# GpSimd refines the reciprocal root of 28 head pairs, and the low half of the first relu stands ahead of a weight join

## The chip, the cores and the metric

The kernel runs on one core of a Trainium2 chip. Its engines are TensorE (PE: matrix multiplications; PEld: loading their weights), VectorE (DVE), ScalarE (ACT), GpSimd (POOL) and SyncE (SP, which here only issues DMAs). Each engine works through its own queue in order; they wait for one another by semaphores. The metric is the device time of one execution in microseconds. Before the change it was 823.23 us, the median of three runs (823.1 to 826.74).

## The reference

Linear attention without softmax, RMS normalisation, then token mixing of rank 32 and a feed-forward network with residuals:

```
kv  = einsum('bhsd,bhse->bhde', k, v)          # 8 batches, 8 heads, 576 rows, 64
out = einsum('bhsd,bhde->bhse', q, kv)
rms = sqrt(mean(out * out, axis=-1) + 1e-06)
x   = out / rms * g_norm                       # heads side by side: 8 x 576 x 512
u   = x + (x^T @ U @ V)^T                      # mixes the 576 rows, rank 32
y   = u + relu(u @ w_ch1) @ w_ch2              # 512 -> 2048 -> 512
```

All in fp32.

## The kernel before, in words

**Products.** An fp32 operand is split into a high half and a low half that TensorE multiplies at its full rate; a product takes three multiplications (high·high, high·low, low·high), each 128x512. The weights of the feed-forward network are split on the way in: a chunk f of them goes through decode steps that the order table calls A, D0, D1, B, D2, H and L. D2 is the join on VectorE (L166, `dec<-raw,top`, 128x1024), H the high half on ScalarE (L260), L the low half on VectorE (L264). `m2D2` is the join of chunk 2.

**Attention.** A step deals with a batch b and a pair of heads p, 32 pairs in all. The four pairs of batch 0 have code of their own (`first_pair`, with its own refinement at L993 to L996, untouched). For the other 28, `stats_parts` (L359 to L373) makes the reciprocal root of the mean square, ten numbers in each of 128 partitions:

- `red` (VectorE): sums of squares; `ta`, `hf` (ScalarE): the root, and −1/2 of the mean square;
- `rc` (VectorE, L370): r0, the reciprocal of the root;
- `na`, `nb`, `nw` (VectorE, L371 to L373): one Newton step, half = (r0·half·r0 + 1.5)·r0.

`mul_step` (VectorE, L384, or L387 for the two heads apart) multiplies the attention output by `half`. From its result TensorE makes the product with U (`t_product`, L410 and L413), and `turn_step` transposes it (VectorE, L400) and sends it through DRAM (`xd`, SP's DMAs at L403 and L405) into the layout of the token mixing, which comes back as `ut` (TensorE L507, VectorE L510, then the split of the row into halves at L451 and L452).

**Feed-forward.** Rows are dealt with in blocks of 512 columns; for a block, chunk f of 16: `ffn1` (L530 to L532) fills a bank `h`, ScalarE makes the high half of its relu (L542, `hh`), VectorE the low half (L547, `hl = max(h, 0) − hh`), and `ffn2` (L554) accumulates. In the first chunks of block 0 there is one bank `h`: chunk f+1 can be begun when the low half of chunk f (`hl0` for chunk 0) has read it. From about 333 us to the end, after three blocks, the rest goes through a Strassen-like scheme (L717, L819, with VectorE's L839 and L841 finishing rows).

**What sets the order.** Up to the end of block 0 two tables (`ORDER0`, `ORDER1`) name every step of that stretch, and each engine's queue has its steps in the order of the table. After that TensorE's order is written out, and that of the other engines comes from a scheduler that simulates the program. The program names a step by letters and the chunk or pair: `f1a` is the first quarter of ffn1 of chunk 1, `hh0` and `hl0` are the relu halves of chunk 0; `na4` is the first refinement step of batch 1's pair 0.

**GpSimd before.** It zeroes buffers at the start, and from then on issues DMAs that store weights to DRAM for the later scheme: a copy `begun<-hh` of 128x1 waits for a chunk's `hh` (L1118 in block 0, L1292 in blocks 1 and 2), three issues of quarters follow (L643, `wd<-ws`), and issues of combinations of weights (L677, `wd<-sh` or `wd<-dec`), which VectorE and ScalarE make at L659, L668, L674 and L675.

Of the kernel before, what the change touches and what calls it, by code (L numbers as in the profile page):

```python
# [16 lines left out]
ALU = mybir.AluOpType  # L17
# [36 lines left out]
tx0 red1 w1B hf1 w1D2 kv3 ta1 t4c0 rc1 w1H t4s0 kv2 nw1 kvb3 w1L wd3 kvb2 mul1 out2 w2A w2D0 out3 lw3 lw2 lw1 sq2 w2D1  # L54
cA tx1 red2 sq3 cD0 ta2 tr1 hf2 red3 t4c1 w2B tr0 rc2 eA t4s1 mix0 nw2 mix1 ta3 cD1 uh0 rc3 mul2 hf3 uh1 nw3 cB tx2
eD0 m2A mul3 tr2 lw4 t4c2 ul1 r0 tx3 t4s2 te0 eD1 sh0 ul0 r1 t4c3 cD2 mix2 te1 tr3 t4s3 cH w2D2 uh2 mix3 m2D0 kv4 uh3
ul2 r3 eB ul3 kvb4 te3 w2H kvc4 f0d eD2 sh1 sh3 m2D1 f0b eH w2L f0c m2B cL f0a eL out4 hh0 m2D2 m3A r2 hl0 m2H m3D0
f1a sq4 f1b m2L te2 f1d lw0 sh2 m3D1 f1c m4A red4 y0 hh1 m4D0 m3B hl1 ta4 m4D1 hf4 f2a m3D2 f2c rc4 m3H sl0 f2d na4
sl1 nb4 sl3 nw4 sl2 f2b mul4 m4B y1 m3L hh2 hl2 m5A m4D2 f3b m5D0 m4H f3a f3d trn4 f3c m4L y2 hh3 m5D1 m6A hl3 m5B
m6D0 f4a m6D1 f4c m5D2 f4b f4d m5H y3 hh4 m5L m6B hl4 m7A m6D2 f5a m7D0 m6H  # L60
# [34 lines left out]
def build(ctx: ExitStack, tc: tile.TileContext, kv_in, kvt0_in, kvt_in, q_in, uv_in, g_in, w_in, out):  # L95
    nc = tc.nc
# [262 lines left out]
    def stats_parts(b, p):  # L359

        NS = 2 * NT
        sums, half, r0, ta = [sm.tile([P, NS], F32, name=n) for n in ("sums", "half", "r0", "ta")]
        xv = state[b, p]["x2"].rearrange("p i (h e) -> p i h e", e=D)
        state[b, p]["r"] = half.rearrange("p (i h) -> p i h", h=2)

        return dict(
            red=lambda: nc.vector.tensor_reduce(out=sums.rearrange("p (i h) -> p i h", h=2), in_=xv, axis=AX.X, op=ALU.add),
            ta=lambda: nc.scalar.activation(out=ta, in_=sums, func=AF.Sqrt, scale=1.0 / D, bias=eps[:, 0:1]),
            hf=lambda: nc.scalar.activation(out=half, in_=sums, func=AF.Identity, scale=-0.5 / D, bias=eps[:, 1:2]),
            rc=lambda: nc.vector.reciprocal(out=r0, in_=ta),  # L370
            na=lambda: nc.vector.tensor_tensor(out=ta, in0=r0, in1=half, op=ALU.mult),  # L371
            nb=lambda: nc.vector.tensor_tensor(out=ta, in0=ta, in1=r0, op=ALU.mult),
            nw=lambda: nc.vector.scalar_tensor_tensor(out=half, in0=ta, scalar=1.5, in1=r0, op0=ALU.add, op1=ALU.mult))  # L373

    def stats_step(b, p):
        for what in stats_parts(b, p).values():
            what()
# [570 lines left out]
    def spread_v(n, eng):  # L948
# [4 lines left out]
        out=uv, in_=uvraw.bitcast(U32).rearrange("p (n t) -> p n t", t=2)[:, :, 1].bitcast(F32), func=AF.Abs)  # L953
# [113 lines left out]
    def second_batch():  # L1067
        own = {}

        def kv():  # L1070
            own["kv"] = [bank()[:, 0:D] for r in range(2)]
            kv_product(1, 0, own["kv"])
            load_kv(1, 1)

        def o():
            out_product(1, 0, (bank(), bank()))
            load_q(1, 1)
            for n, what in stats_parts(1, 0).items():
                step[f"{n}4"] = what

        step.update(kv4=kv, kvb4=lambda: kv_move(1, 0, own["kv"]), kvc4=lambda: kv_add(1, 0, own["kv"]), out4=o, sq4=lambda: squares(1, 0),
                    mul4=lambda: mul_step(1, 0), trn4=lambda: turn_step(1, 0))
# [55 lines left out]
    def stretch(name, before, now, after):  # L1138
# [17 lines left out]
        def o():  # L1156
            out_product(*now, (place("one"), place("two")))
            behind_turn(load_q, *now)
            new_steps(squares_parts(*now))
            new_steps(stats_parts(*now))  # L1160
# [230 lines left out]
```

## Time and profile before

| | |
|---|---|
| median of three runs | 823.23 us (823.1 to 826.74) |
| span of the profiled execution | 820.8 us |
| TensorE busy | 812.3 us, 99% |
| VectorE busy | 590.0 us, 72% |
| ScalarE busy | 438.9 us, 53% |
| GpSimd busy | 83.0 us, 10% |

The page has no time of the profiled execution beside its span; the median of the runs is 2.4 us above the span. An engine's busy time counts the union of its instructions, DMA issues among them for GpSimd. A matmul's end is modelled, so that consecutive ones overlap in a timeline: a 128x512 one is shown with 0.39 us and the next begins 0.23 us after it.

### The profile page before, as it was taken

What the parts mean: (1) busy time and instruction counts of PE and PEld (TensorE: products, weight loads), DVE (VectorE), ACT (ScalarE), POOL (GpSimd) and SP (SyncE); (2) the same over time, 40 slices, a digit from 0 to 9 for tenths busy, and PEclk for the clock granted to TensorE, in tenths of its full rate; (3) what the DMA queues carried; (4) which work ended last, traced back from release to release, by engine and by line L of the source; (5) the groups of instructions that cost most, each with busy time, mean ns of one, the idle gap of its engine ahead of it and who ended that gap; (6) DMA issues with size and microseconds to landing.
All of it is one profiled execution on the core that took longest, in us unless ns stands there. A gap on an engine that the chain in (4) does not pass through costs nothing.

```text
span 820.8 us, 15247 instructions
## 1 busy us (share of the span) xinstructions
PE 812.3 (99%) x5940; PEld 669.8 (82%) x5940; DVE 590.0 (72%) x1044; ACT 438.9 (53%) x782; POOL 83.0 (10%) x159
## 2 busy tenths in 40 slices
PE   9899999999999999999999999999999999999998
PEld 8688888878888888888888888888888888888887
DVE  5999995887876788558867688678538933682376
ACT  6869773344433545456645664656246624543462
POOL 3002232345321221000000000000000000000000
PEclk9999999999999999999999999999999999999999
DMA  9985778788896777577778768675555675555554
GB/s 344 415 352 162 231 238 259 256 272 269 271 318 226 240 254 233 167 264 246 251 241 287 230 212 294 222 246 196 193 205 193 204 272 202 206 179 186 199 205 154
DMA packets 64824, 196.87 MB, mean 240 GB/s; under 512 B 8176, under 2 KB 25840, under 8 KB 54000
## 3 DMA queue, kind: packets, MB, share of 16 engines
q1 hardware_dynamic: 55648, 166.40, 59.7%
q0 software_dynamic: 8960, 29.37, 10.6%
q8 instruction: 47, 0.77, 0.4%
q14 instruction: 25, 0.20, 0.1%
q10 hardware_dynamic: 144, 0.13, 0.0%
HBM read 145.27 MB, written 50.59 MB: 239 GB/s over the span
## 4 chain that ended last, share of the span: by engine, by line
PE 93%; DVE 4%; DMA 1%; issue 1%; ACT 1%; POOL 0%; SPq 0%; DVEq 0%; ACTq 0%; POOLq 0%
PE yy L717 28%; PE yy L819 26%; PE y L554 15%; PE h L530 5%; PE h L531 5%; PE h L532 5%; PE ya L769 2%; PE pp L313 1%; PE pp L333 1%; PE h L859 1%; PE h L313 1%; DMA wd<-dec 1%; PE pp L410 1%; DMA q_sb<-q_in 1%; PE big L333 1%
## 5 line engine op out<-in xcount | busy, mean ns | idle before, releaser
L717 PE MATMUL yy<-uc,wt 128*128 128x512 f32 x1008 | 233.5, 391 | 0.0
L717 PEld LDWEIGHTS yy<-uc,wt 128*128 128x128 f32 x1008 | 188.2, 188 | 39.3
L819 PE MATMUL yy<-dec,wt 128*128 128x512 f32 x468 | 113.7, 391 | 0.0
L554 PE MATMUL y<-hh,ws 128*128 128x512 f32 x336 | 113.1, 394 | 0.0
L819 PE MATMUL yy<-hh,wt 128*128 128x512 f32 x312 | 103.4, 391 | 0.0
L819 PEld LDWEIGHTS yy<-dec,wt 128*128 128x128 f32 x468 | 87.4, 188 | 18.2
L708 DVE TENSOR_TENSOR hl<-hk,hh 128x512 fp32r<-128x512 f32 x72 | 48.1, 687 | 43.9 <-ACT hh L747 43.7
L708 DVE TENSOR_TENSOR dec<-hk,dec 128x512 fp32r<-128x512 f32 x72 | 49.0, 687 | 36.9 <-ACT dec L747 36.5
L554 PEld LDWEIGHTS y<-hh,ws 128*128 128x128 f32 x336 | 63.1, 188 | 13.6
L819 PEld LDWEIGHTS yy<-hh,wt 128*128 128x128 f32 x312 | 58.6, 188 | 12.2
L530 PE MATMUL h<-ut,ws 128*128 128x512 f32 x168 | 66.5, 396 | 0.0
L531 PE MATMUL h<-ut,ws 128*128 128x512 f32 x168 | 65.6, 390 | 0.0
L532 PE MATMUL h<-ut,ws 128*128 128x512 f32 x168 | 65.6, 390 | 0.0
L554 PE MATMUL y<-hl,ws 128*128 128x512 f32 x168 | 65.5, 390 | 0.0
L819 PE MATMUL yy<-hl,wt 128*128 128x512 f32 x156 | 60.8, 390 | 0.0
L747 ACT CAST dec<-hk 128x512 fp32r<-128x512 f32 x72 | 44.2, 620 | 30.5 <-PE yy L819 15.6
L747 ACT CAST hh<-hk 128x512 fp32r<-128x512 f32 x72 | 44.1, 622 | 27.5 <-PE yy L819 22.9
L705 ACT COPY sp<-yy 128x1024 f32<-128x1024 f32 x35 | 35.5, 1014 | 35.5 <-PE yy L717 27.5
L730 ACT ACTIVATE hk<-hk 128x1024 f32<-128x1024 f32 x24 | 25.5, 1061 | 37.7 <-DVE hk L729 37.6
L542 ACT ACTIVATE hh<-h 128x512 fp32r<-128x512 f32 x48 | 28.4, 591 | 30.7 <-PE h L532 30.6
L547 DVE SCALAR_TENSOR_TENSOR hl<-h,hh 128x512 fp32r<-128x512 f32 x48 | 32.8, 683 | 10.1 <-ACT hh L542 9.8
L532 PEld LDWEIGHTS h<-ut,ws 128*128 128x128 f32 x168 | 31.6, 188 | 6.8
(246 smaller groups left out, 1349.5 us busy)
## 6 DMA issues: line engine op xcount, KB each, us to landing
wt<-wd SPq DMA_DIRECT2D x84, 1024.0 KB, 4.9
kv_sb<-kv_in SPq DMA_DIRECT2D x29, 512.0 KB, 6.1
raw<-w_in SPq DMA_DIRECT2D x14, 1023.6 KB, 15.4
wd<-dec POOLq DMA_DIRECT2D x44, 256.0 KB, 5.0
wd<-ws POOLq DMA_DIRECT2D x42, 256.0 KB, 4.8
q_sb<-q_in SPq DMA_DIRECT2D x29, 288.0 KB, 5.9
ut<-xd SPq DMA_DIRECT2D x28, 288.0 KB, 4.5
out<-x SPq DMA_DIRECT2D x23, 256.0 KB, 4.5
```

The lines of the kernel that those rows point to most:

```text
L530: nc.tensor.matmul(h, lhsT=w1s[f][0][:, d, :], rhs=uh[d], start=(n == 0), stop=False)
L531: nc.tensor.matmul(h, lhsT=w1s[f][0][:, d, :], rhs=ul[d], start=False, stop=False)
L532: nc.tensor.matmul(h, lhsT=w1s[f][1][:, d, :], rhs=uh[d], start=False, stop=(n == ND - 1))
L542: last["relu"] = nc.scalar.activation(out=last["hh"], in_=h, func=AF.Relu)
L547: last["low"] = nc.vector.scalar_tensor_tensor(out=hl, in0=h, scalar=0.0, in1=last["hh"].bitcast(F32), op0=ALU.max, op1=ALU.subtract)
L554: nc.tensor.matmul(acc, lhsT=w2s[f][w][:, c, :], rhs=h[:, cols], start=(f == 0 and w == 0 and h is hh), stop=(f == NF - 1 and w == 1))
L705: last["unit"] = nc.scalar.copy(out=pair_bank("P6") if name == "P1" else spare(name), in_=acc)
L708: return nc.vector.tensor_tensor(out=out, in0=a, in1=b, op=ALU.subtract)
L717: nc.tensor.matmul(acc[:, i], lhsT=w[:, ws_, e * P:(e + 1) * P], rhs=u[:, e, us], start=name in ("P1", "P5") and e == 0 and k == 0, stop=e ...
L730: last["unit"] = nc.scalar.activation(out=to, in_=to if other else acc, func=AF.Relu)
L747: last["unit"] = nc.scalar.copy(out=hh, in_=src)
L819: nc.tensor.matmul(acc[:, c], lhsT=w[:, ws_, c * P:(c + 1) * P], rhs=h, start=name in ("P1", "P5") and kk == 0 and i == 0, stop=kk == KEEP ...
```

## The change

Two edits. In `ORDER0`, `hl0` moves from behind `m2D2 m3A r2` to directly behind `hh0`. In `stats_parts`, `na` and `nb` go from VectorE to GpSimd, and `nw`, one VectorE operation that adds 1.5 and multiplies by r0, becomes two GpSimd operations. The lines of the kernel behind L373 have a number higher by one after the change.

```diff
-ul2 r3 eB ul3 kvb4 te3 w2H kvc4 f0d eD2 sh1 sh3 m2D1 f0b eH w2L f0c m2B cL f0a eL out4 hh0 m2D2 m3A r2 hl0 m2H m3D0
+ul2 r3 eB ul3 kvb4 te3 w2H kvc4 f0d eD2 sh1 sh3 m2D1 f0b eH w2L f0c m2B cL f0a eL out4 hh0 hl0 m2D2 m3A r2 m2H m3D0
...
             rc=lambda: nc.vector.reciprocal(out=r0, in_=ta),
-            na=lambda: nc.vector.tensor_tensor(out=ta, in0=r0, in1=half, op=ALU.mult),
-            nb=lambda: nc.vector.tensor_tensor(out=ta, in0=ta, in1=r0, op=ALU.mult),
-            nw=lambda: nc.vector.scalar_tensor_tensor(out=half, in0=ta, scalar=1.5, in1=r0, op0=ALU.add, op1=ALU.mult))
+            na=lambda: nc.gpsimd.tensor_tensor(out=ta, in0=r0, in1=half, op=ALU.mult),
+            nb=lambda: nc.gpsimd.tensor_tensor(out=ta, in0=ta, in1=r0, op=ALU.mult),
+            nw=lambda: (nc.gpsimd.tensor_scalar(out=ta, in0=ta, scalar1=1.5, scalar2=None, op0=ALU.add),
+                        nc.gpsimd.tensor_tensor(out=half, in0=ta, in1=r0, op=ALU.mult)))
```

TensorE's order stays as it is. VectorE's queue at the first chunk, before (L921 is the end of the weights of chunk 0, L166 the join m2D2, L547 hl0, L264 the low half of chunk 2's weights):

```order
L921 TENSOR_TENSOR w2s_563<-dec,w2s_563 128x512
L166 SCALAR_TENSOR_TENSOR dec<-raw_206,top 128x1024
L547 SCALAR_TENSOR_TENSOR hl<-h,hh 128x512
L155 TENSOR_SCALAR dec<-dec 128x256
L156 TENSOR_SCALAR dec<-dec 128x1024
L264 TENSOR_TENSOR ws_613<-dec,ws_613 128x1024
```

and after the change:

```order
L922 TENSOR_TENSOR w2s_563<-dec,w2s_563 128x512
L548 SCALAR_TENSOR_TENSOR hl<-h,hh 128x512
L166 SCALAR_TENSOR_TENSOR dec<-raw_206,top 128x1024
L155 TENSOR_SCALAR dec<-dec 128x256
L156 TENSOR_SCALAR dec<-dec 128x1024
L264 TENSOR_TENSOR ws_613<-dec,ws_613 128x1024
```

The low half now stands ahead of the join, and nothing else moves there. GpSimd's queue in block 0 around the stores that follow the copy at 109 us, before:

```order
L1118 COPY begun<-hh 128x1
L643 DMA wd_117<-ws_722 128x2x256
L643 DMA wd_119<-ws_722 128x2x256
L643 DMA wd_120<-ws_780 128x2x256
L1118 COPY begun<-hh 128x1
```

and after, with the refinement of pair (1,3) (its r0 is r_1375):

```order
L1119 COPY begun<-hh 128x1
L644 DMA wd_117<-ws_723 128x2x256
L644 DMA wd_119<-ws_723 128x2x256
L644 DMA wd_120<-ws_781 128x2x256
L371 TENSOR_TENSOR ta<-r_1375,half 128x10
L372 TENSOR_TENSOR ta<-ta,r_1375 128x10
L373 TENSOR_SCALAR ta<-ta 128x10
L374 TENSOR_TENSOR half<-ta,r_1375 128x10
L1119 COPY begun<-hh 128x1
```

The four operations stand behind three DMA issues. In block 1, at pair (3,0) (r_2433), GpSimd's queue before:

```order
L1292 COPY begun<-hh 128x1
L643 DMA wd_135<-ws_1275 128x2x256
L643 DMA wd_138<-ws_1345 128x2x256
L643 DMA wd_141<-ws_1345 128x2x256
L677 DMA wd_125<-sh 128x512
L677 DMA wd_126<-sh 128x512
```

and after:

```order
L371 TENSOR_TENSOR ta<-r_2433,half 128x10
L1293 COPY begun<-hh 128x1
L644 DMA wd_135<-ws_1277 128x2x256
L644 DMA wd_138<-ws_1348 128x2x256
L644 DMA wd_141<-ws_1348 128x2x256
L372 TENSOR_TENSOR ta<-ta,r_2433 128x10
L678 DMA wd_125<-sh 128x512
L678 DMA wd_126<-sh 128x512
L373 TENSOR_SCALAR ta<-ta 128x10
L374 TENSOR_TENSOR half<-ta,r_2433 128x10
```

The copy and five issues now stand between the four operations of one pair. VectorE's queue at the same pair, after, from its reciprocal to its multiplication (L385):

```order
L370 RECIPROCAL r_2433<-ta 128x10
L548 SCALAR_TENSOR_TENSOR hl<-h,hh 128x512
L676 TENSOR_TENSOR sh<-st,sh 128x2x256
L548 SCALAR_TENSOR_TENSOR hl<-h,hh 128x512
L660 TENSOR_TENSOR st<-ws_813 128x512
L660 TENSOR_TENSOR st<-ws_893 128x512
L669 TENSOR_TENSOR st<-st 128x256
L385 TENSOR_TENSOR x_88<-x_88,half 128x640
```

Before, the multiplication and the transposition stood ahead of the second `hl` there; now that `hl`, both L660 and an L669 stand ahead of it.

## Rows read from the trace of the kernel before

**Rows 1.** The page: busy time, share and count of each engine; the chain's shares by engine.
```profile
PE 812.3 (99%) x5940; PEld 669.8 (82%) x5940; DVE 590.0 (72%) x1044; ACT 438.9 (53%) x782; POOL 83.0 (10%) x159
...
PE 93%; DVE 4%; DMA 1%; issue 1%; ACT 1%; POOL 0%; SPq 0%; DVEq 0%; ACTq 0%; POOLq 0%
```

**Rows 2.** Busy time in two stretches: start:end, length, then busy us of each engine.
```profile
0.00:36.70 36.70, 31.88 (x328) 27.59 (x328) 27.07 (x76) 26.31 (x65) 6.43 (x31) 1.00 0.97 375
36.70:820.80 784.10, 780.46 (x5612) 642.17 (x5612) 562.93 (x970) 412.55 (x718) 76.56 (x128) 1.00 0.70 234
```

**Rows 3.** The chain of waits from 30 to 62 us: start, us, what.
```profile
36.11 0.61 DVE hl L547
...
36.77 0.50 PE h L530
```

**Rows 4.** Timeline, ScalarE, VectorE, TensorE: start, us, engine, line, operation, shapes, [idle before].
```profile
34.70 0.60 ACT L542 ACTIVATE hh<-h 128x512 fp32r<-128x512 f32 x1
...
34.89 1.22 DVE L166 SCALAR_TENSOR_TENSOR dec<-raw,top 128x1024 uint32<-128x1024 uint32 x1
...
41.01 0.68 DVE L547 SCALAR_TENSOR_TENSOR hl<-h,hh 128x512 fp32r<-128x512 f32 x1
...
42.31 0.39 PE L530 MATMUL h<-ut,ws 128*128 128x512 f32 x1
```

**Rows 5.** Groups by line and form, VectorE, one of three alike.
```profile
L371 DVE TENSOR_TENSOR ta<-r,half 128x10 f32<-128x10 f32 x28 | 4.7, 168 | 1.4
```

**Rows 6.** Timeline, GpSimd's copy alone and beside a VectorE join.
```profile
77.08 0.18 POOL L1118 COPY begun<-hh 128x1 f32<-128x1 f32 x1 [4.03 <-ACT hh L542]
...
95.16 1.22 DVE L166 SCALAR_TENSOR_TENSOR dec<-raw,top 128x1024 uint32<-128x1024 uint32 x1
...
95.44 0.97 POOL L1118 COPY begun<-hh 128x1 f32<-128x1 f32 x1 [4.35 <-ACT hh L542]
```

**Rows 7.** Timeline around pair (1,0), VectorE and TensorE.
```profile
43.41 0.21 DVE L370 RECIPROCAL r<-ta 128x10 f32<-128x10 f32 x1
...
44.43 0.89 DVE L387 TENSOR_TENSOR x<-pp,half 128x320 f32<-128x320 f32 x2
...
46.37 0.69 DVE L547 SCALAR_TENSOR_TENSOR hl<-h,hh 128x512 fp32r<-128x512 f32 x1
...
47.75 0.39 PE L530 MATMUL h<-ut,ws 128*128 128x512 f32 x1
```

**Rows 8.** Timeline around pair (1,3), GpSimd, VectorE, TensorE.
```profile
109.93 2.17 POOL L643 DMA_DIRECT2D wd<-ws  x3
...
111.73 0.82 DVE L384 TENSOR_TENSOR x<-x,half 128x640 f32<-128x640 f32 x1
...
128.61 0.82 DVE L510 TENSOR_TENSOR ut<-pp,ut 128x288 f32<-128x288 f32 x2 [5.41 <-DMA ut<-xd]
...
130.94 0.47 PE L531 MATMUL h<-ut,w1s 128*128 128x512 f32 x1
```

**Rows 9.** Timeline around pair (3,0), GpSimd, VectorE, TensorE.
```profile
197.16 0.82 DVE L384 TENSOR_TENSOR x<-x,half 128x640 f32<-128x640 f32 x1
...
198.28 0.43 PE L410 MATMUL pp<-x,uf 128*32 128x128 f32 x8
...
199.35 1.27 DVE L659 TENSOR_TENSOR st<-ws 128x512 f32<-128x512 f32 x2
...
199.56 1.12 POOL L677 DMA_DIRECT2D wd<-sh  x2 [0.51 <-DVE hl L547]
...
200.66 1.56 DVE L668 TENSOR_TENSOR st<-st 128x256 f32<-128x256 f32 x4
```

**Rows 10.** Timeline at 421 us, VectorE and TensorE.
```profile
421.27 0.83 DVE L384 TENSOR_TENSOR x<-x,half 128x640 f32<-128x640 f32 x1
...
422.01 1.27 DVE L839 SCALAR_TENSOR_TENSOR x<-x,g_sb,yy 128x1024 f32<-128x1024 f32 x1
...
422.82 0.43 PE L410 MATMUL big<-x,uf 128*32 128x128 f32 x8
```

## The prediction

> **What bounds the kernel now.** I read the page's first part first, then its chain, then the busy time by stretch, then the timelines around each place that the change touches. The first row shows TensorE busy for 812.3 us of a span of 820.8 us, VectorE for 590.0 us, ScalarE for 438.9 us and GpSimd for 83.0 us; the chain of work that ended last is TensorE for 93% of the span and VectorE for 4% [rows 1]. The table of stretches says where the 4% lie: up to 36.70 us TensorE works 31.88 us, and in the 784.10 us behind that it works 780.46 us, at a granted clock of 1.00 [rows 2]. So from the second FFN chunk on all that can be won is 784.10 − 780.46 = 3.6 us, and every delay that reaches TensorE is paid in full, for there is no later idle time in which it is made good. VectorE's 72% is an average and is no bound anywhere after 36.70 us; what matters of it is when its queue, which runs in order, lets single results out.
>
> The last VectorE piece of the chain is the low half of the first relu, 36.11 to 36.72 us, and TensorE's second chunk starts at 36.77 us [rows 3]: the bank `h` is free for chunk 1 only when hl0 has read it.
>
> **Part 1, hl0 ahead of m2D2.** The high half hh0 runs on ScalarE from 34.70 for 0.60 us, so it ends at 35.30; the join m2D2 starts on VectorE at 34.89 for 1.22 us, and hl0 stands behind it [rows 4]. In the new order hl0 starts at hh0's end plus the 0.05 us that a hand-over takes in rows 3 (36.72 to 36.77), so near 35.35, and ends near 36.0 instead of 36.72: TensorE's chunk 1 starts some 0.7 us sooner. But VectorE, which is back to back here, now idles from 34.9 until 35.35 for hh0, some 0.45 us, and the join starts at 35.95 and not at 34.89. All that stands behind it on VectorE (one decode step, then the low half of chunk 2's weights after ScalarE's high half of them) is late by 0.3 to 0.7 us, down to hl1, which ran at 41.01 for 0.68 us. hl1 lets TensorE begin chunk 2 at 42.31, 0.62 us after hl1's end [rows 4]; with TensorE 0.7 us early and hl1 0.7 us late, hl1 would end at 42.4 and chunk 2 begin near 42.45: +0.14 us. The gain is spent one chunk later. Its bounds are −0.7 (hl1 doesn't slip) and +0.3 (it slips by a whole 0.9).
>
> **Part 2, what goes.** Three VectorE instructions for each of 28 pairs go, 84 in all; the first kind takes 168 ns (28 of them 4.7 us), the other two read alike [rows 5], so 84 × 0.168 = 14.1 us of VectorE's 590.0. VectorE isn't the bound after 36.70 us, so this is worth nothing in itself.
>
> **Part 2, what comes.** Four GpSimd operations of 128x10 for each pair, and two hand-overs between engines (the reciprocal to GpSimd, `half` back to VectorE's multiplication), where before there was none. The trace has no GpSimd arithmetic of this size. The nearest row is the copy of 128x1: 0.18 us when undisturbed, 0.97 us when it starts at 95.44 beside a VectorE join that runs from 95.16 for 1.22 us [rows 6]. The copy then ends at 96.41, 0.03 us after the join ends at 96.38: it seems to have been held until the join was over. So one operation costs 0.18 to 0.97 us. I take 0.25, near the undisturbed end, because at the places that count below VectorE itself stands waiting for the result, and there is nothing beside which to be held. A chain is then 4 × 0.25 + 3 × 0.05 between them + 2 × 0.05 hand-overs = 1.25 us, against 0.5 on VectorE, and the multiplication that waits for it holds all of VectorE's queue. In most pairs the reciprocal stands 0.7 us or more ahead of the multiplication, with other work between, and TensorE's consumer is microseconds later; those I cost at nothing. Four places are different.
>
> On the copy's two prices the Trainium skill bears: "GPSIMD Engine Reference", § 8 Key points, says that GpSimd shares its SBUF interfaces with VectorE and contends with VectorE instructions that have two SBUF inputs, and that elementwise work is structurally about twice as fast on VectorE. The 0.97 beside a join of two SBUF inputs agrees with the first. By the second an operation would be 2 × 0.168 = 0.34 us (an estimate from that page's factor), and a chain 1.6 us instead of 1.25.
>
> *Pair (1,0), 43 us.* The reciprocal runs from 43.41 for 0.21 us and the multiplications start at 44.43; hl2 stands behind them at 46.37 (0.69 us) and TensorE's chunk 3 follows at 47.75 [rows 7]. The chain ends at 43.62 + 1.25 = 44.87, so multiplication, weights and hl2 are 0.45 us later. In the new order these are already late by part 1. hl2's end has 0.69 us to TensorE; a slip of 0.45 on top of 0.7 uses it up and passes 0.45 on: **+0.45** (0 to +1).
>
> *Pair (1,3), 110 us.* On GpSimd the four operations stand behind a copy and three DMA issues of the weight stores; the issues run from 109.93 for 2.17 us, until 112.10. The chain ends near 113.3; the multiplication was at 111.73: +1.55 us. From it the result goes through the transposition, SP's DMAs to and from DRAM, and comes back for the token mixing, at 128.61, before which VectorE waited 5.41 us for the DMA; two operations later TensorE begins the row at 130.94, which is the second matmul group of block 1 and takes 0.47 us in place of its usual 0.39 because it already waits a little [rows 8]. So all of it arrives: **+1.5** (0.5 if VectorE's order makes some of it good, 2.5 if the operations cost 0.5).
>
> *Pair (3,0), 197 us.* Here GpSimd's order puts the copy, three store issues and two `sh` issues between the four operations. The two `sh` issues run from 199.56 for 1.12 us, until 200.68; the last two operations end near 201.25. The multiplication was at 197.16 and lasts 0.82, and TensorE uses its result at 198.28, 0.3 us after its end [rows 9]. That is 4.1 − 0.3 = +3.8 us. VectorE's new order sets a floor: the multiplication now stands behind two operations of L659 (1.27 us together) and one of L668 (1.56 for four) [rows 9], 1.66 us, so at least +1.4. The issues wait in the program on semaphores of earlier DMAs, which need not slip by the 2.1 us that TensorE is late by then; if they don't, 3.8 − 2.1 = 1.7. I take the middle of 1.7 and 3.8: **+2.8** (1.4 to 5.9, where GpSimd has a further 2 us of issues to wait for).
>
> *421 us.* VectorE's new order puts L839 (1.27 us, at 422.01) ahead of the multiplication at 421.27, whose result TensorE takes at 422.82 [rows 10]. If L839's input is ready by 421.3 the multiplication ends at 423.3 (+0.5); if only at 422.01, at 424.0 (+1.2). I take **+0.9**.
>
> The sum is 0.14 + 0.45 + 1.5 + 2.8 + 0.9 = +5.8 us on a span of 820.8. The median of the runs is 823.23, 2.4 us over that span; I add the difference to it: **829.0 us**. The sum by the factor of the page would be 0.35 more at each of the first three places of part 2, so 830.
>
> **Rivals.**
> *The delays are mostly absorbed.* GpSimd's queue runs ahead of TensorE: its DMA issues wait for earlier DMAs, not for TensorE, and if these are through in time the pair (3,0) costs only VectorE's floor, 1.4, and pair (1,3) 0.5; with 0.6 for the rest that is +2.5: 825.7 us. For it: GpSimd is busy for 10% only [rows 1]. Against: the three issues at 109.93 follow right behind hh and can't be sooner.
> *Faster, VectorE relieved.* At the start of the FFN the 0.7 us of part 1 are kept and the 14.1 us less on VectorE let the queue catch up, so that some waits of TensorE for it go too: −0.7 − 0.5 = 822.0; the floor is −0.7 − 3.6, 818.9 [rows 2]. It decides if GpSimd's chain ends before VectorE's queue reaches the multiplication in every one of the places above. Against it: at 109.93 to 112.10 GpSimd is occupied by issues while the multiplication was due at 111.73 [rows 8].
> *Held operations.* If each GpSimd operation is held to the end of the VectorE instruction beside it, as the copy at 95.44 was, it costs 0.7 to 0.97 and a chain 3 to 4 us. That adds some 2 us at the three places of pairs above and uses up the spare time at some two or three others in blocks 0 and 1: 5.8 + 5 × 2 = +16, **839 us**. Against: once VectorE stands at the multiplication nothing holds GpSimd. By the first rule of the page above this would be the general case.
>
> **How the numbers follow.** The forecast, +3.5 to +10 us (826.7 to 833), has 0.60; absorbed delays 0.22; held operations 0.13; faster 0.05. A measurement here can tell 0.5%, 4.1 us, from no change: 819.1 to 827.3. The absorbed rival is within that, and a small piece of the forecast; the faster one splits. Faster by over 0.5% 0.02, within it 0.26, slower 0.72. The range leaves out the faster case and the far end of the held one: 824.3 to 840.
>
> **What would show it.** After: hl0 at about 35.35 and TensorE's chunk 1 at about 36.1; chunk 2 at 42.3 to 42.5 all the same. GpSimd's operations of 128x10 at 0.2 to 0.35 us. New idle time of VectorE before the multiplications with GpSimd as releaser, near 44.4, 112 and 199 us; new idle time of TensorE before the row of block 1 that stood at 130.94, before L410 near 200 and near 424. TensorE busy still 812. It is wrong if block 1 starts no later than before, if TensorE finds the result of (3,0) ready, or if the 128x10 operations take over 0.5 us each.

## The result, and the profile after

The changed kernel takes 832.23 us (median of four runs, 831.0 to 835.03), the kernel before 824.12 us beside it (823.1 to 826.74): a ratio of 1.011 with a 95% interval of 1.0088 to 1.0132, slower by 7 to 11 us. The profiled executions have spans of 829.2 and 820.8 us, 8.4 us apart. The forecast was 829.0 us, 5.8 us more than before; the medians are 8.1 us apart.

The page of the kernel after, first part and chain, answering to [rows 1]:

```profile
PE 815.1 (98%) x5940; PEld 670.0 (81%) x5940; DVE 579.2 (70%) x960; ACT 438.9 (53%) x782; POOL 117.5 (14%) x271
...
PE 80%; DMA 6%; DVE 5%; ACT 3%; issue 2%; POOL 2%; SPq 1%; ACTq 0%; POOLq 0%; DVEq 0%
```

VectorE has lost 10.8 us of work and GpSimd has gained 34.5 us; the chain, which was TensorE for 93%, now has 80%, with VectorE, ScalarE, GpSimd and DMAs in the rest: TensorE waits for others in the middle of the program. Where, a comparison of the start of each TensorE instruction in the two traces shows. Its delay against before grows in steps (the delay just behind a place, less that just ahead of it):

| at (before, us) | what starts late | step, us | forecast |
|---|---|---|---|
| 36.8 | chunk 1 | −0.67 | −0.7 |
| 42 | chunk 2 | +0.93 | +0.84 |
| 47.8 | chunk 3, behind pair (1,0) | +0.48 | +0.45 |
| 114 | product of (1,3) | +0.32 | in 1.5 |
| 131 | row of block 1, behind (1,3) | +0.59 | in 1.5 |
| 157, 178 | waits of before are shorter or gone | −0.58 | none |
| 198 | product of (3,0) | +4.11 | +2.8 |
| 198.3 to 200.2 | the work right behind it, slower | +1.50 | none |
| 423 | product at 421 us's pair, (6,1) | +0.82 | +0.9 |
| 429, 523 | waits in the last stage | +0.45 | none |

They sum to 7.95 us; with steps under 0.1 us, and a chunk 0 that ended 0.13 us sooner than before, the last instruction has a delay of 8.14 us. The first three steps in the timeline of VectorE and TensorE after (columns as in [rows 4]):

```profile
35.20 0.69 DVE L548 SCALAR_TENSOR_TENSOR hl<-h,hh 128x512 fp32r<-128x512 f32 x1 [0.35 <-ACT hh L543]
...
35.81 1.22 DVE L166 SCALAR_TENSOR_TENSOR dec<-raw,top 128x1024 uint32<-128x1024 uint32 x1
...
41.61 0.68 DVE L548 SCALAR_TENSOR_TENSOR hl<-h,hh 128x512 fp32r<-128x512 f32 x1
...
42.35 0.50 PE L531 MATMUL h<-ut,ws 128*128 128x512 f32 x1 [0.65 <-DVE hl L548]
...
48.26 0.50 PE L531 MATMUL h<-ut,ws 128*128 128x512 f32 x1 [0.18 <-DVE hl L548]
```

hl0 ran at 35.20 (36.03 before), the join behind it at 35.81 (34.89), hl1 at 41.61 (41.01); chunk 2 waited 0.65 us for it. The new refinement of pair (1,0), with the multiplication that waits for it, against [rows 7]:

```profile
44.00 0.21 DVE L370 RECIPROCAL r<-ta 128x10 f32<-128x10 f32 x1
...
44.39 0.24 POOL L371 TENSOR_TENSOR ta<-r,half 128x10 f32<-128x10 f32 x1 [33.30 <-DVE r L370]
...
45.00 0.25 POOL L373 TENSOR_SCALAR ta<-ta 128x10 f32<-128x10 f32 x1
...
45.34 0.21 POOL L374 TENSOR_TENSOR half<-ta,r 128x10 f32<-128x10 f32 x1
...
45.58 0.89 DVE L388 TENSOR_TENSOR x<-pp,half 128x320 f32<-128x320 f32 x2 [0.87 <-POOL half L374]
```

Four operations of 0.21 to 0.25 us with starts 0.3 us apart; the wait of VectorE, 0.87 us, stands in the last row. In the other 27 pairs GpSimd's first operation has this distribution (minimum/median/maximum in ns):

```profile
L371 POOL TENSOR_TENSOR ta<-r,half x27: 196/207/1066, 80.8 to 566.8; 128x10 f32<-128x10 f32 x27
```

So 0.21 us is the rule, and single first operations take up to 1.07 us (over all 112 operations the median is 0.21, the mean 0.31 and the longest 1.25 us). At pair (1,3), against [rows 8]:

```profile
111.08 2.17 POOL L644 DMA_DIRECT2D wd<-ws  x3
...
114.19 0.21 POOL L374 TENSOR_TENSOR half<-ta,r 128x10 f32<-128x10 f32 x1
...
114.43 0.82 DVE L385 TENSOR_TENSOR x<-x,half 128x640 f32<-128x640 f32 x1 [1.56 <-POOL half L374]
...
130.29 0.82 DVE L511 TENSOR_TENSOR ut<-pp,ut 128x288 f32<-128x288 f32 x2 [4.01 <-DMA ut<-xd]
```

The chain stood behind the three issues, and VectorE waited 1.56 us for it. At pair (3,0), against [rows 9]:

```profile
195.50 0.20 POOL L371 TENSOR_TENSOR ta<-r,half 128x10 f32<-128x10 f32 x1 [1.34 <-DVE r L370]
...
196.47 1.47 POOL L644 DMA_DIRECT2D wd<-ws  x2 [0.39 <-issue]
...
199.28 0.73 POOL L644 DMA_DIRECT2D wd<-ws  x1 [1.34 <-issue]
...
199.43 0.43 DVE L669 TENSOR_TENSOR st<-st 128x256 f32<-128x256 f32 x1
...
200.03 0.22 POOL L372 TENSOR_TENSOR ta<-ta,r 128x10 f32<-128x10 f32 x1
...
200.84 1.12 POOL L678 DMA_DIRECT2D wd<-sh  x2 [0.58 <-issue]
...
201.98 0.26 POOL L373 TENSOR_SCALAR ta<-ta 128x10 f32<-128x10 f32 x1
...
202.32 0.21 POOL L374 TENSOR_TENSOR half<-ta,r 128x10 f32<-128x10 f32 x1
...
202.56 0.82 DVE L385 TENSOR_TENSOR x<-x,half 128x640 f32<-128x640 f32 x1 [2.70 <-POOL half L374]
...
203.53 0.61 PE L411 MATMUL pp<-x,uf 128*32 128x128 f32 x8 [4.04 <-DVE x L385]
```

The reader sees the queue that the order announced: operation, three issues, operation, two issues, two operations, 7 us for a chain that takes 1.2 us when it stands together. The multiplication waited 2.70 us for its last link and TensorE 4.04 us. VectorE had its last work before that (199.43 + 0.43) over at 199.86; the multiplication of before, at 197.16 plus TensorE's delay of 1.14, would have been at 198.3. So VectorE's new order alone would have made it 1.6 us late, and GpSimd's chain, which ended last, made it 4.3 us late. What follows is slower too, by stretches (columns as in [rows 2], the granted clock third from the end):

```profile
199.10:203.53 4.43, 0.39 (x2) 0.03 (x1) 1.69 (x4) 0.00 (x0) 2.54 (x6) 1.00 0.79 282
203.53:206.59 3.06, 3.06 (x89) 2.77 (x89) 2.88 (x6) 1.24 (x2) 0.56 (x1) 0.52 0.15 34
206.59:209.60 3.01, 3.01 (x14) 2.56 (x13) 0.71 (x4) 2.74 (x8) 1.67 (x4) 0.92 0.78 245
```

In the 3.06 us behind the wait the granted clock is 0.52, TensorE's level of 1.2 GHz for nearly all of it, and 1.00 before. The 1.50 us of the step behind (3,0) are that.

At pair (6,1), against [rows 10], GpSimd wasn't what VectorE waited for:

```profile
428.37 1.28 DVE L840 SCALAR_TENSOR_TENSOR x<-x,g_sb,yy 128x1024 f32<-128x1024 f32 x1 [0.88 <-PE yy L820]
...
428.40 0.20 POOL L374 TENSOR_TENSOR half<-ta,r 128x10 f32<-128x10 f32 x1
...
429.57 0.82 DVE L385 TENSOR_TENSOR x<-x,half 128x640 f32<-128x640 f32 x1
```

The chain was over at 428.60; the multiplication stood behind L840 in VectorE's new order, and L840 had waited 0.88 us for TensorE. The 0.82 us there are VectorE's order.

### The profile page after: what moved, and what is told of

It is laid out like the page before. It is cut to its first block, busy times and chain, and to the rows that moved or that the text cites. A ratio compares the mean times of both kernels' runs of the same rounds, so it can differ in the third digit from the quotient of the medians.

```text
span 829.2 us, 15275 instructions
## 1 busy us (share of the span) xinstructions
PE 815.1 (98%) x5940; PEld 670.0 (81%) x5940; DVE 579.2 (70%) x960; ACT 438.9 (53%) x782; POOL 117.5 (14%) x271
## 4 chain that ended last, share of the span: by engine, by line
PE 80%; DMA 6%; DVE 5%; ACT 3%; issue 2%; POOL 2%; SPq 1%; ACTq 0%; POOLq 0%; DVEq 0%
PE yy L718 28%; PE yy L820 25%; PE y L555 10%; PE h L531 3%; PE h L532 3%; PE h L533 3%; DMA raw<-w_in 3%; PE ya L770 2%; DVE dec L166 1%; PE pp L313 1%; DMA temps<-kvt_in 1%; DVE ws L264 1%; PE pp L333 1%; DMA wf<-dec 1%; POOL wd L644 1%
## 5 line engine op out<-in xcount | busy, mean ns | idle before, releaser
L709 DVE TENSOR_TENSOR dec<-hk,dec 128x512 fp32r<-128x512 f32 x72 | 48.9, 686 | 36.8 <-ACT dec L748 36.3
L371 POOL TENSOR_TENSOR ta<-r,half 128x10 f32<-128x10 f32 x28 | 9.6, 344 | 308.1 <-DVE r L370 264.9
L548 DVE SCALAR_TENSOR_TENSOR hl<-h,hh 128x512 fp32r<-128x512 f32 x48 | 32.8, 683 | 11.0 <-ACT hh L543 10.8
```

The lines of the kernel that those rows point to most:

```text
L548: last["low"] = nc.vector.scalar_tensor_tensor(out=hl, in0=h, scalar=0.0, in1=last["hh"].bitcast(F32), op0=ALU.max, op1=ALU.subtract)
L709: return nc.vector.tensor_tensor(out=out, in0=a, in1=b, op=ALU.subtract)
```

## The experiments

| run | ratio to before (95%) |
|---|---|
| hl0 ahead alone | 1.0004 (0.9991 to 1.0017) |
| refinement on GpSimd alone | 1.0113 (1.0081 to 1.0145) |
| four pairs back on VectorE | 1.0015 (1.0003 to 1.0027) |
| stores behind (3,0)'s refinement | 1.0049 (1.0033 to 1.0065) |
| only (3,0) on GpSimd | 1.0074 (1.0058 to 1.0090) |
| stores behind (1,3)'s as well | 1.0035 (1.0016 to 1.0054) |

The theory: the loss is made at a few places where GpSimd's chain stands behind DMA issues, or where VectorE's queue has no spare time. The rivals: each of the 28 moved refinements costs a little; GpSimd's latency costs it wherever it stands; hl0's move has a part in it.

**hl0 ahead alone.** The edit of `ORDER0`, with the refinement on VectorE.

> Before with the one edit of ORDER0 (hl0 ahead of m2D2); the refinement stays on VectorE. Theory (gain spent one chunk later): chunk 1 of TensorE starts some 0.7 us sooner, chunk 2 is on time or 0.1 to 0.2 us late, end of the span +0.1 to +0.4 us, ratio 0.999 to 1.002. Rival (hl0's gain is kept and the other edit hides it): span 0.7 us shorter. Rival (the reordering itself costs several us downstream): +2 us or more.

Ratio 1.0004: no change. Its trace shows the gain and its return (TensorE's step −0.68 at chunk 1, +0.96 at chunk 2):

```profile
35.77 0.69 DVE L547 SCALAR_TENSOR_TENSOR hl<-h,hh 128x512 fp32r<-128x512 f32 x1 [0.35 <-ACT hh L542]
...
42.17 0.68 DVE L547 SCALAR_TENSOR_TENSOR hl<-h,hh 128x512 fp32r<-128x512 f32 x1
...
42.91 0.50 PE L530 MATMUL h<-ut,ws 128*128 128x512 f32 x1 [0.68 <-DVE hl L547]
```

The wait for the first low half has become a wait of 0.68 us for the second. The median can't tell ±0.7 us, so the rival of a kept gain falls by the trace, not by the time. The span of this trace is 1.4 us over before's where 0.1 to 0.4 was expected: another 1.06 us comes at 523 us, in the last stage; it isn't followed further.

**Refinement on GpSimd alone.** Only the edit in `stats_parts`.

> The refinement of the 28 pairs on GpSimd alone; ORDER0 as before. Theory: nearly all of the loss, span +7.5 to +8.5 us over before's 820.8, ratio 1.009 to 1.011; steps of TensorE's delay at (1,0) near +0.4, (1,3) +0.9, (3,0) +5.5, (6,1) +0.9. Rival (the two edits need each other): half of it or less, under +4 us.

Ratio 1.0113, as large as the whole change; the interval reaches to 1.0145. Its one profiled execution is longer than that, 834.1 us, with waits of its own near 96 to 114 us (2.7 us in three steps) and small ones later that were not followed further; the step at (3,0) is +4.72, and the clock's on top +1.49. At (1,0) the expected +0.4 did not come: the step is +0.02.

```profile
45.62 0.89 DVE L388 TENSOR_TENSOR x<-pp,half 128x320 f32<-128x320 f32 x2 [0.88 <-POOL half L374]
...
48.40 0.40 PE L531 MATMUL h<-ut,ws 128*128 128x512 f32 x1
```

VectorE waits for GpSimd as in the changed kernel, but TensorE starts chunk 3 without a wait. So the +0.48 of the changed kernel needs both edits: hl0's move has used up the spare time behind hl2, 0.69 us in [rows 7]. The rest of the loss comes with this edit alone.

**Four pairs back on VectorE.**

```diff
-            na=lambda: nc.gpsimd.tensor_tensor(out=ta, in0=r0, in1=half, op=ALU.mult),
+            na=lambda: (nc.vector if (b, p) in ((1, 0), (1, 3), (3, 0), (6, 1)) else nc.gpsimd).tensor_tensor(...)
...
```

(`nb` and `nw` alike.)

> The changed kernel with the pairs (1,0), (1,3), (3,0) and (6,1) refined on VectorE as before, and the other 24 on GpSimd. Theory (the loss is made at four places and the rest is hidden): span within 1 us of before's 820.8, ratio 0.998 to 1.002. Rival (every GpSimd refinement costs a little, by hand-overs or by holding VectorE's reads): 24/28 of the loss stays, +7 us, ratio 1.008.

Ratio 1.0015: 1.2 us of some 9 are left with 24 of 28 pairs on GpSimd. TensorE does the product of (3,0) on time:

```profile
198.24 0.39 PE L556 MATMUL y<-hh,ws 128*128 128x512 f32 x1
...
198.55 0.42 PE L412 MATMUL pp<-x,uf 128*32 128x128 f32 x8
```

The rival of a small cost at each pair asked for 7 us and falls. The ratio is within what was expected; the span, 822.6, is 1.8 us over before's where 1 was the limit, mostly in three steps of 0.4 to 0.5 us, at 157, 199 and 304 us.

**Stores behind (3,0)'s refinement.** All 28 pairs on GpSimd; the copy and the three issues of chunk 9 of block 1 are queued behind the last refinement operation.

```diff
                 if n == SPREAD[j, f][0]:
-                    last["stores"] = nc.gpsimd.tensor_copy(...)
+                    with tc.issue_after(last[3, 0].ins) if (j, f) == (1, 9) else ExitStack():
+                        last["stores"] = nc.gpsimd.tensor_copy(...)
```

> The changed kernel, with the copy and the weight stores of chunk 9 of block 1 queued on GpSimd behind the whole refinement of pair (3,0), so that its four operations stand together; all 28 pairs still on GpSimd. Theory (the place in GpSimd's queue costs 5.5 of the 8.1 us): span +2.3 to +3.2 us over before, ratio 1.003 to 1.004, no idle time of TensorE at (3,0) over 0.5 us and the granted clock 1.00 there. Rival (latency of the GpSimd operations and hand-overs costs it wherever they stand): +7 us or more.

Ratio 1.0049, 4.0 us (2.7 to 5.4) in place of 9: the place in the queue, with the clock that its wait costs, is worth some 5 us. The expected 2.3 to 3.2 was the low side: its trace loses 3.3 us from chunk 1 to the end, nearly all at the other places. Ahead of that it has 4.65 us more of start-up, which the refinement doesn't touch: TensorE's granted clock was 0.50 there. At (3,0):

```profile
199.63 0.20 POOL L375 TENSOR_TENSOR ta<-r,half 128x10 f32<-128x10 f32 x1 [0.93 <-DVE r L374]
...
200.53 0.21 POOL L368 TENSOR_TENSOR half<-ta,r 128x10 f32<-128x10 f32 x1
...
204.71 0.43 PE L414 MATMUL pp<-x,uf 128*32 128x128 f32 x8
```

```profile
204.80:206.80 2.00, 1.98 (x89) 1.68 (x89) 1.97 (x5) 0.00 (x0) 1.31 (x2) 1.00 0.84 252
```

The chain takes 1.1 us, TensorE doesn't wait, and the clock stays at 1.00. With the chain together the scheduler also put VectorE's multiplication back ahead of `hl`, so the run doesn't separate GpSimd's queue from VectorE's. In the changed kernel's trace VectorE stood waiting for GpSimd's last operation for 2.70 us; a run with the issues between the operations and VectorE's old order, which would price the two apart, was not made.

**Only (3,0) on GpSimd.** The other 27 and `ORDER0` as before.

> Before, with the refinement of the one pair (3,0) on GpSimd; the other 27 and ORDER0 as before. Theory (one place makes two thirds of the loss): TensorE waits 3 to 4.5 us for the multiplication of (3,0), loses some 1.5 us more at half the granted clock, span +4.5 to +6 us, ratio 1.005 to 1.007. Rival (the place counts only because TensorE and the issues of GpSimd have been shifted against each other by the 2.1 us lost earlier): under +2.5 us.

Ratio 1.0074, 6.1 us (4.8 to 7.4), and 5.5 us in its trace: one pair of 28 makes two thirds of the loss. TensorE waits 3.56 us and then runs at a lower clock again (0.59 in the next 3 us); the rival, that the place counts only after earlier delays, falls.

```profile
202.25 0.43 PE L412 MATMUL pp<-x,uf 128*32 128x128 f32 x8 [3.56 <-DVE x L386]
```

```profile
202.20:205.20 3.00, 2.95 (x89) 2.77 (x90) 2.92 (x6) 1.29 (x3) 0.46 (x1) 0.59 0.18 40
```

**Waits of a chosen length.** The refinement of all pairs on VectorE as before; 4, 9 or 14 GpSimd multiplications of `half` by 1.0 stand between it and the multiplication of (3,0), and the copy and stores of chunk 9 of block 1 are queued behind them, as above. Each was run once, so only the traces are read. (With 9 and 14 the scheduler also put `hl` and some `st` operations ahead of the multiplication on VectorE; TensorE's wait is measured, and includes what that costs.)

```diff
+            for _ in range(9 if (b, p) == (3, 0) else 0):
+                last[b, p] = nc.gpsimd.tensor_scalar(out=half, in0=half, scalar1=1.0, scalar2=None, op0=ALU.mult)
```

> Before (refinement of all pairs on VectorE), with 4 GpSimd multiplications of half by 1.0 between the refinement and the multiplication of pair (3,0), and the next stores behind them: a wait of TensorE of known size at one place. Theory (each GpSimd operation costs 0.33 us there, and the granted clock falls only in a wait of several us): TensorE waits 1 to 2 us, granted clock 1.00 behind it, total +1 to +2. Rival (every wait of over 1 us costs clock): clock under 0.8 behind it and 1 us more.

> As the run with 4, with 9 such multiplications: TensorE waits 2.5 to 3.7 us. Theory: if the clock falls as after the wait of 4.04 us of the changed kernel, the 1.5 us come on top; if it stays at 1.00, the fall needs a longer wait. I lean to no fall.

> As the run with 4, with 14 such multiplications: TensorE waits 4.3 to 5.5 us. Theory: granted clock 0.5 for 2 to 3 us behind the wait, 1.2 to 1.8 us lost on top of it. Rival (the fall in the changed kernel came from elsewhere, not from the wait): clock 1.00, nothing on top.

TensorE's first instruction behind the wait, and the 3 us from there on, for 4, 9 and 14:

```profile
200.83 0.43 PE L415 MATMUL pp<-x,uf 128*32 128x128 f32 x8 [1.53 <-DVE x L389]
```

```profile
200.80:203.80 3.00, 2.97 (x93) 2.66 (x94) 2.96 (x6) 0.00 (x0) 1.40 (x2) 1.00 0.73 225
```

```profile
201.91 0.43 PE L415 MATMUL pp<-x,uf 128*32 128x128 f32 x8 [3.20 <-DVE x L389]
```

```profile
201.90:204.90 3.00, 2.99 (x93) 2.66 (x94) 2.74 (x7) 1.34 (x4) 1.38 (x2) 1.00 0.71 230
```

```profile
202.76 0.65 PE L415 MATMUL pp<-x,uf 128*32 128x128 f32 x8 [4.38 <-DVE x L389]
```

```profile
202.70:205.70 3.00, 2.94 (x88) 2.80 (x88) 2.61 (x5) 1.24 (x2) 2.10 (x4) 0.50 0.75 215
205.70:208.70 3.00, 3.00 (x15) 2.32 (x10) 0.70 (x3) 2.25 (x7) 1.52 (x3) 0.53 0.91 311
```

The run with 9 has a second long wait, in a late stage that its nine operations don't touch:

```profile
530.79 0.47 PE L722 MATMUL yy<-uc,wt 128*128 128x512 f32 x1 [3.35 <-issue]
```

```profile
530.80:533.80 3.00, 3.00 (x8) 2.37 (x9) 2.93 (x5) 1.58 (x2) 0.00 (x0) 0.56 0.26 109
```

Waits of 1.53 and 3.20 us at (3,0) left the clock at 1.00 and cost TensorE just themselves (steps of +1.60 and +3.27). The wait of 4.38 us was followed by 0.50 and 0.53, and cost 2.57 us on top of its +4.45, more than the 1.2 to 1.8 expected; the one of 3.56 (only (3,0)) 1.46, that of 4.04 (the change) 1.50, and the late one of 3.35, with 0.56 behind it, 1.7. So the fall follows the wait, and what it adds differs. The total of the run with 9 isn't read, for the late wait and its slower clock make 5.2 us of it.

The length of one wait isn't all that decides. In the start-up of the run with the stores behind (3,0)'s refinement, TensorE waited 1.24 us until 23.79, as it did for 1.1 to 1.25 us in all the other traces, and there alone the clock fell behind it:

```profile
25.00:38.00 13.00, 13.00 (x77) 10.76 (x77) 10.24 (x22) 7.06 (x17) 0.00 (x0) 0.50 1.02 419
```

Two more runs, only (3,0) and that with 4 multiplications, have some 3 us at 0.50 in the start-up, behind a wait of 0.8 us that the kernel before has too, at 1.00. What was different is open.

**Stores behind (1,3)'s as well.** In addition `g12`, the copy and issues of chunk 12 of block 0, behind the refinement of (1,3).

```diff
-... m14D2 hfD g12 y11b naD hl12
-m14H nbD m15D1 pu2 pv2 f13a nwD av2 m15B muD f13b ...
+... m14D2 hfD y11b naD hl12
+m14H nbD m15D1 pu2 pv2 f13a nwD av2 m15B g12 muD f13b ...
...
+            with tc.issue_after(last[1, 3].ins) if f == 12 else ExitStack():
```

> As the run with the stores of chunk 9 of block 1 behind the refinement of (3,0), and the copy and stores of chunk 12 of block 0 behind that of (1,3) as well. Theory (at (1,3) the three issues ahead of the four operations cost it, 0.9 us in the trace of the changed kernel): no step of TensorE's delay at the product of (1,3), under 0.2 us at block 1's row; ratio 1.003 to 1.005, some 0.9 us under the run with one place mended. Rival (the hand-overs cost it): both steps stay, 0.4 and 0.5 us.

Half of it held. The step at the product of (1,3) is gone; the step at block 1's row is still +0.55. Its ratio, 1.0035, and that of the run with one place mended can't be told apart. Its trace loses 1.40 us at (3,0), where the other run lost 0.26, though GpSimd's chain was together and over at 196.20: VectorE's multiplication stood behind an `sh` operation whose input ScalarE made only when an earlier store had landed (a wait of 2.26 us), and 0.84 us more came behind the product, where TensorE waited 0.61 us for a load. So with the stores behind, that place isn't always free. VectorE at the multiplication:

```profile
112.03 0.40 POOL L368 TENSOR_TENSOR half<-ta,r 128x10 f32<-128x10 f32 x1
...
113.22 0.46 DVE L514 TENSOR_TENSOR ut<-pp,ut 128x288 f32<-128x288 f32 x1 [0.86 <-DMA ut<-xd]
...
113.59 0.81 DVE L388 TENSOR_TENSOR x<-x,half 128x640 f32<-128x640 f32 x1
```

GpSimd's chain was over at 112.43; the multiplication now stood behind a mixing operation that waited 0.86 us for another transfer from DRAM. So the 0.59 us at block 1's row is not shown to be GpSimd's: the four kernels with (1,3) on GpSimd (the change and this one among them) all have a step of 0.55 to 0.98 there, but so has one of the six with it on VectorE, the one with 14 multiplications (+0.55).

No version beat the kernel before. The 0.68 us of hl0, had they been kept, would be less than these times can tell.

## Why the prediction was right, and where not

- *hl0 ahead.* −0.7 and then +0.84 were forecast, −0.67 and +0.93 came. VectorE idles for hh0 (0.35 us for the 0.45 forecast) and hands the delay on through the join to hl1, as forecast.
- *Nothing for the 84 removed operations.* Right: the 84 add up to the 14.1 us forecast (10.8 us of busy time, which counts overlapping ends once), and TensorE gains nothing but the 0.58 us at 157 and 178 us, which the run with hl0 alone shows too (−0.51), without any GpSimd refinement. Those are waits of before that took up delays made earlier.
- *GpSimd's operation at 0.25 us.* Right: 0.20 to 0.26 at the places that count. The rival of held operations has its mechanism in single operations (1.25 us at most, and a mean of 0.31 for a median of 0.21) but not its place: VectorE stands waiting there. By the page "GPSIMD Engine Reference" of the Trainium skill, § 8 Key points, an elementwise operation would be about twice VectorE's 0.168; at these ten elements the trace has 0.21, 1.25 times it.
- *(1,0), and 421 us.* +0.45 and +0.9 forecast, +0.48 and +0.82 measured, the second by the order that the forecast named (L840, its L839, ahead of the multiplication). That the slip at (1,0) reaches TensorE only on top of part 1's is borne out: without hl0's move the step is +0.02.
- *(1,3).* The multiplication was to be 1.55 us late and was 1.93 (114.43 against 111.73, less TensorE's delay of 0.77), but "all of it arrives" failed: 0.91 us arrived, and of that only the 0.32 at the product is shown to be GpSimd's. The load of `ut` was issued 2.78 us later than before (125.83 for 123.05) but landed only 1.68 us later (130.29 for 128.61), with TensorE 1.1 us late by then: the way through DRAM took up the rest.
- *(3,0).* The mechanism was right, the size wrong in two terms. The wait was put at 2.8, the middle of 1.7 and 3.8, and came out at 4.11: the two `sh` issues ran at 200.84 for 199.56, so GpSimd's issues slipped with TensorE's delay of 1.14 after all. And the granted clock had no term: 1.50 us. TensorE's busy time, which was to stay at 812, rose to 815.1 us, half of it by that. The floor of 1.66 us for VectorE's new order came out at 1.56 by luck: it left out the `hl` that stands ahead of the multiplication too, and the `sh` ahead of that `hl` ran at 196.41 for 196.55, 1.3 us sooner against TensorE.
- *The rest.* The 0.45 at 429 and 523 us were not foreseen. At 523 us runs without any GpSimd refinement have larger steps (+1.06 with hl0 alone, +0.89 with 14 multiplications), so the 0.25 there isn't shown to be the change's; the 0.20 at 429 is in no other trace and stays open.

The terms that were named sum to +5.8, and measured in the same places to 6.58 (−0.67 + 0.93 + 0.48 + 0.91 + 4.11 + 0.82); the clock's 1.50 is most of the difference to 8.14. The absorbed rival (+2.5) failed at (3,0). The faster one failed at three places, where VectorE waited 0.87, 1.56 and 2.70 us for GpSimd; at (6,1) its condition held, the chain ended before VectorE came, and 0.82 us were lost all the same to VectorE's new order.

## What to carry to other kernels

Before an operation moves to an engine that is "10% busy", look at what stands ahead of it in that engine's queue at the places where someone waits for the result: here three and two DMA issues turned a chain of 1.2 us into 7. Where the busiest engine is at 99%, freeing another one is worth nothing, and each place where the result has no spare time must be found one by one; of 28, four held nearly all of the loss (1.2 us was left without them) and one cost two thirds. If the operation must move, queue the issues behind it: here that brought 9 us down to 4, though not to nothing. And look at what the scheduler does to the other queues: at (6,1) VectorE's new order alone made the loss.

## What the runs showed of the hardware

A long wait can cost more than itself. Behind TensorE's waits of 3.35, 3.56, 4.04 and 4.38 us the granted clock stood at 0.56, 0.59, 0.52 and 0.50 for the next 3 us, and 1.46 to 2.57 us were lost on top; behind 1.53 and 3.20 us it stayed at 1.00. But in one start-up it stood at 0.50 for the 13 us shown above, behind a wait of 1.24 us. The Trainium skill, "TensorE: Matmul & The Clock Gate", § What's actually happening, says that the lower of the two levels is the default and activity releases it. These traces agree in part: the higher level came back only after TensorE had worked at the lower one, but waits of up to 3.20 us left the higher one alone, and behind the wait of 3.56 us the first 0.3 us of work still ran at 1.00, before the fall.
